# One more pair of heads turned by VectorE and through DRAM, the weights' shift also on ScalarE, and a new order

## The chip, the core and the metric

The kernel runs on one core of a Trainium2 chip. The metric is the time on the device of one execution, in microseconds; the kernel before takes 916.67 us, the median of three runs (916.0 to 917.14). A core has a matrix engine (TensorE, PE in the profile; PEld is its loading of weights), three elementwise engines (VectorE or DVE, ScalarE or ACT, GpSimd or POOL) and SyncE (SP), which issues the transfers between DRAM and the core's memory here. Each engine works through its own instructions in the order in which the program has them, and waits on semaphores for the others.

## What is computed

```python
scores = scale * np.matmul(q, k.transpose(0, 1, 3, 2))       # 8 batches, 8 heads, 576 x 576, head size 64
thresh = np.max(scores, axis=-1, keepdims=True) - tau
scores = np.where(scores >= thresh, scores, -1000000000.0)
attn = np.exp(scores - np.max(scores, axis=-1, keepdims=True))
attn = attn / (np.sum(attn, axis=-1, keepdims=True) + 1e-09)
x = heads_joined(np.matmul(attn, v))                          # 8 x 576 x 512
x_prev = shifted_by_one_position(x)
xk = mu_k * x + (1.0 - mu_k) * x_prev
xr = mu_r * x + (1.0 - mu_r) * x_prev
k = np.maximum(xk @ w_k, 0.0)                                 # 512 -> 1024
v = k * k @ w_v                                               # 1024 -> 512
out = v / (1.0 + np.exp(-(xr @ w_r)))
```

All is in 32 bit. The weights `w_k`, `w_v` and `w_r` come as 64-bit floats and are made into 32-bit ones on the chip.

## The kernel before

**Attention.** Work goes by batch `b` and by pair of heads `hp`, 0 to 3. Queries of a pair are cut into four units of 128 (`P`, both heads) and one of the last 64 queries of both heads (`T`). A unit has score matmuls (L656, or L628 and L639), then for each head a row maximum on VectorE (L740), the threshold from it (one tiny instruction on ScalarE L748, VectorE L756 or GpSimd L761), the exponential on ScalarE (L768), the mask with its sum on VectorE (L776), and a scaling by 1 / sum on GpSimd (L812) or ScalarE (L816). The probabilities `p` must then be turned so that keys lie along the partitions. There are two ways for that. In `turn_pair` and `turn_last`, a pair that isn't `moved` is turned by TensorE: 128x128 transposes (L830), 9 for a unit `P` and 5 for the unit `T`, and copies out of PSUM into `pm` (L845 on ScalarE, L846 on VectorE). A pair that is `moved` is turned in blocks of 32x32 by VectorE (L865, L878 and, for the unit `T`, L928) into `pt`, which is written to DRAM (`far`, `near`, `end`) and read back in another order into `pm`. The value matmuls (`attend`, L1017) follow: for a pair turned by TensorE once for each half of the queries, for a moved one both halves together. In the kernel before the pairs of batches 2 to 7 are moved, those of batches 0 and 1 aren't. The values `v` have one buffer.

**Feed-forward.** When four pairs are done, chunks of 256 positions go through `ffn_chunk`: mixing on GpSimd and ScalarE, matmuls with `w_k` (L1211), `w_r` (L1262) and `w_v` (L1285), each as three products of high and low parts. These matmuls are what TensorE has to do between the pieces of attention.

**Weights.** `weight` turns one of 20 pieces of 128x512 from 64 to 32 bits: GpSimd clamps the high words, ScalarE scales them (L451), VectorE shifts the low words right by 29 bits into a PSUM bank (L459) and joins the two (L467, L477), and two more steps split the result into parts for TensorE. The last shift starts at 159 us.

**Order.** All steps are first collected in a list. A table of numbers (`PLACES`) gives each step its place in one common order, from which each engine's own order and the buffers follow; another (`PICKS`) chooses, for each step that several engines can do, which one does it.

```python
eng, occ, fn = ((eng, occ, fn), *alt)[next(self.picks)]
self.out = sorted(range(len(steps)), key=place.__getitem__)
```

Of the kernel before, what the change touches and what calls it, by code (L numbers as in the profile page):

```python
# [26 lines left out]
    "!z!v!|!{#%#*#D#M#O#<#B#6#J#T#[#$#.#/#7#2#9#5#C#;#F#W#}$1$:$!$+#j#s#R#Y$J$N$O$S$V$[!/!R%W#A#U#K#V#P#X#`#f#c#i#{#~$I$T",
    "#n#x$($5$2$@#r#_#z$%$#$-#e#q#k#u$8$=$z$~$g$x$,$<$`$c%,%2%4%F%K%c!Z#?&<#S#]#t$9$4#|#o$$$.$6#y$D$K$H$P$&$3$/$7$Y${%+%B",
    "$p$t$l%8$k$n$A$X$L$R$Q$W$b$i$h$o%b%o%|&!$r%$%&%:%=%N&,&/&1&6&:&K$_%3%U%g*K%9%I%V&c()(8(^)T)q(J(i)S){*0*6*=*F*L*Q*U*W",
    "*e+D+m+r,),1,4,:,k,o,r,{-:-@.:.T*@*J*O*]*a*g*q*z+,+w-k.v-v-z-}.+.U.^.c.e.m.w/</C+4+;+>+M+V*u*|+(+C+Q,Y/Q/_/b/h0P0^0b",  # L30
    "1E1L1_0y0}1%11191G1u1{2%2T$*$e(3$m$w$}%#%(%E%S%@%L$a$d$f$j$s$q$u%7%<%M%]%f&$%}%j%p%s$v$y$|%%%!%-%*%0%)%1%.%5%?%G%P%_",
    "%r&&%T%`&E&G%>%D%6%;%H%X%R%Y%A%O%J%Q%n%v&i&l%l%w%~&?%e%k&x(#(&(-(/(T(Y%/%h))%{&+&0&H&X&T&2&8&B%Z%^%a%i%u%q%z&C&N&R&`",
    "&Z&g&d&k&n&u%t%y&%&(&#&*&-&3&.&5&7&=&f($(1(6&A&U&M&_&h&t&;&@&F&I&D&S&L&V&P&Y&W&b&q&z(A(X&{(2&s&|(](d(o(s(y(|)%);)=&O",
    "(()z(.(5(<(C(H(M(=(W(e&^&a&e&j&r&w(+(Q(v)>)L(I).(n(E(K(L(4(7&m&o(>(D(F(N&v&}(!(,(m(u)#),(_(g(:(?(j(x(V(a(;(@(h(q(r)$",
    "(G(O(P([)6)?)G)K)7)C)3)8)*)0)`*2*#(R)2+s)9)F)[)U)Z)h)n)r)u(c(f(k(w(})!)()g)o*[*c)A)P)M)Q)i)d)-)/)4):)5)B)<)D)@)I)E)O",
    ")e)l*/*<)R)Y)v)|)W)_)J)N)X)])V)c)a)p)b)k)m)t*1*R*o*}*;*>***.)}*&+],5,,1e+1,/,K,W--,7/O0U0]0e0p1g2C2O0w1$1P2!2t3)3-31",
    "3M3V3^3t3}4(4.432;2]2_2b2j3$3>3O4:4<4C4F2.222?2P2e2v3#35383B3K3Q3+333<3@3G3J3R3U3`3e3h3m3g3j3o3v4+4$4e4f4w5<5@5)5.53",
    "56595C5I5Z5x6<4U4Z4`4r4}5=5O5T5]6@*!*^-^*k+B+&+b*s,!+^+l+f)x)~*$*-*5*3*:*M+-+9+U+h+Z+I+L+O*+*8*C*E*?*G*H*X*I*V*P*_*h",
    "*m+%*p+/+5+#+*+:+=*`*f*j*l*i*w*r+$*t+7+!+<+P+X+d+i+q+{,+,<+x,$,J,d,t+++2+F+J+6+?+@+H+Y+g+_+j+u+z+~,(,?,I,8,@,0,2+v+y",
    "+S+W,%,3,.,9+a+n+k+t,F,O,S,V,Z,c,j,},^,`-/-D+N,D/A,[,i,x,y-.-E-K-Y-S+},#,&,-,;,6,>,L,b,h,z-#-%,q-9-8,E,G,A,B,M,U,R,]",  # L40
    ",H,P,N,T,m,u-,-4-C-J-G-m-=-P,e,g,_,a,l,s,v,~,f,p,n,w-(-2-;-B-R-W-]-g-V-`.8.P.X-!-$-&-+-*-3-1-5-0-7-6-?-I-M-X-_-f-|-n",
    "-s-y..-L-O->-A-T-c-[-d-F-U-Q-Z-j-o-w-r.!.*.(./.5.;.x/:-).30_.?.F.i.}/&/5.V.G.z-l-q-t-{.&.%.,.9.@.K.W.u/1.[.g.f-b-h.-",
# [1409 lines left out]
```

## Time and profile before

| | before |
|---|---|
| median of 3 runs | 916.67 us (916.0 to 917.14) |
| the profiled execution's own time | 915.72 us |
| its span, first to last instruction | 914.0 us |
| TensorE busy | 902.3 us, 99% |
| VectorE busy | 715.5 us, 78% |
| GpSimd busy | 666.5 us, 73% |
| ScalarE busy | 598.5 us, 65% |
| granted TensorE clock | 1.00 over the span |

Busy time is the time in which an engine has an instruction in work. Matmuls overlap one another, so a mean duration of one is longer than the time from one start to the next. The chain of waits is followed back from the last instruction, at each step to what released it. A line of the program (L865) is that of `kernel.py` of the run. In a transfer, the time to landing counts from its issue to its last byte.

### The profile page before, as it was taken

How to read it: one execution, taken by the hardware profiler on the slowest of the kernel's cores; microseconds unless marked ns; L12 is line 12 of the kernel's file. 1: busy time of each engine (PE TensorE's matmuls, PEld its weight loads, DVE VectorE, ACT ScalarE, POOL GpSimd, SP SyncE). 2: the span in 40 equal slices, each digit the busy share in tenths (PEclk: the TensorE clock that was granted, in tenths of full speed). 3: DMA queues.
4: the chain of work that ended last, by engine and by line, in shares of the span. 5: the costliest groups of instructions: out<-in, count | busy, mean ns of one | idle time of the engine just before them, and what ended most of it. 6: DMA issues, size and time to landing. Idle time of an engine off the chain costs nothing.

```text
span 914.0 us, 17624 instructions
## 1 busy us (share of the span) xinstructions
PE 902.3 (99%) x5970; PEld 744.1 (81%) x5970; DVE 715.5 (78%) x1615; ACT 598.5 (65%) x1154; POOL 666.5 (73%) x824
## 2 busy tenths in 40 slices
...
GB/s 332 276 217 246 105 106 119 145 305 308 334 296 311 313 320 322 301 323 313 299 297 272 315 252 321 305 321 320 296 321 291 281 310 261 238 131 24 24 24 23
DMA packets 146249, 226.60 MB, mean 248 GB/s; under 512 B 20080, under 2 KB 82672, under 8 KB 146160
## 3 DMA queue, kind: packets, MB, share of 16 engines
...
HBM read 108.27 MB, written 73.14 MB: 198 GB/s over the span
## 4 chain that ended last, share of the span: by engine, by line
PE 84%; DVE 9%; ACT 4%; issue 1%; POOL 1%; ACTq 0%; DVEq 0%; POOLq 0%
PE w L1211 21%; PE w L1285 20%; PE w L1017 15%; PE s L656 12%; PE w L1262 9%; DVE p L776 3%; DVE sm L740 3%; PE s L628 3%; PE w L830 2%; PE s L639 2%; ACT p L768 2%; ACT pm L845 1%; DVE pt L865 1%; PE w L1378 0%; DVE r L1161 0%
## 5 line engine op out<-in xcount | busy, mean ns | idle before, releaser
L768 ACT ACTIVATE p<-s,sm 128x576 f32<-128x576 f32 x288 | 209.6, 738 | 122.8 <-DVE sm L740 100.0
L776 DVE SCALAR_TENSOR_TENSOR p<-s,sm,p 128x576 f32<-128x576 f32 x288 | 230.9, 811 | 32.4 <-ACT p L768 19.7
L740 DVE TENSOR_REDUCE sm<-s 128x1 f32<-128x576 f32 x288 | 213.2, 750 | 42.4 <-PE s L656 30.4
L1211 PE MATMUL w<-xk,wk 128*128 128x256 f32 x1728 | 227.5, 281 | 0.0
L1211 PEld LDWEIGHTS w<-xk,wk 128*128 128x128 f32 x1728 | 215.8, 188 | 4.1 <-issue 1.7
L1285 PE MATMUL w<-wv,k 128*128 128x512 f32 x864 | 218.0, 395 | 0.0
L1285 PEld LDWEIGHTS w<-wv,k 128*128 128x128 f32 x864 | 157.6, 188 | 31.2 <-ACT raw L529 0.4
L1017 PE MATMUL w<-pm,v 128*64 128x256 f32 (+1 forms) x1280 | 164.9, 409 | 0.0
L1017 PEld LDWEIGHTS w<-pm,v 128*64 128x64 f32 x1280 | 88.1, 137 | 64.0 <-issue 5.8
L865 DVE STREAM_TRANSPOSE pt<-p 128x1024 f32<-128x1024 f32 x96 | 117.8, 1228 | 8.0 <-POOL p L812 5.0
L812 POOL TENSOR_SCALAR p<-p,sm 128x576 f32<-128x576 f32 x119 | 89.2, 753 | 39.0 <-DVE sm L801 36.7
L1243 POOL TENSOR_TENSOR k<-r,k 128x512 fp32r<-128x512 f32 x72 | 93.0, 1294 | 31.0 <-ACT k L1224 28.4
L816 ACT ACTIVATE p<-p,sm 128x576 f32<-128x576 f32 x133 | 101.3, 771 | 20.2 <-DVE sm L801 19.8
L1262 PE MATMUL w<-wr,xk 128*128 128x512 f32 x432 | 112.4, 395 | 0.0
L656 PE MATMUL s<-st 128*128 128x288 f32 x480 | 107.9, 308 | 1.9 <-DVE p L776 1.6
L567 POOL TENSOR_TENSOR hl<-raw,hl 128x640 fp32r<-128x640 f32 (+1 forms) x64 | 97.9, 1539 | 14.3 <-ACT hl L550 7.8
L656 PE MATMUL s<-st,st 128*128 128x288 f32 x480 | 102.2, 296 | 0.0
L656 PEld LDWEIGHTS s<-st 128*128 128x128 f32 x480 | 78.3, 189 | 20.4 <-DVE p L776 8.3
L1262 PEld LDWEIGHTS w<-wr,xk 128*128 128x128 f32 x432 | 77.5, 188 | 13.8
L656 PEld LDWEIGHTS s<-st,st 128*128 128x128 f32 x480 | 77.2, 188 | 1.9
L1220 ACT ACTIVATE r<-r 128x512 f32<-128x512 f32 x72 | 45.4, 631 | 34.8 <-DVE r L1219 33.7
L1291 DVE TENSOR_TENSOR sg<-w,sg 128x512 f32<-128x512 f32 x36 | 24.0, 680 | 44.8 <-PE w L1285 40.9
...
## 6 DMA issues: line engine op xcount, KB each, us to landing
far<-pt SPq DMA_DIRECT2D x96, 576.0 KB, 4.2
pm<-far SPq DMA_DIRECT2D x48, 1152.0 KB, 7.3
...
v<-in_v SPq DMA_DIRECT2D x36, 320.0 KB, 4.0
...
```

The lines of the kernel that those rows point to most:

```text
L567: lambda cs=cs: G.tensor_tensor(hl.get()[:, 1, cs], raw.get()[:, cs], hl.get()[:, 0, cs].bitcast(F32), op=ALU.subtract),
L656: PE.matmul(ss[y].get()[:, z, 0:HS], l.get()[:, c * P : (c + 1) * P], r[:, z * HS : (z + 1) * HS], start=(j == 0), stop=(j == 1),)
L740: lambda sv=sv, col=col: V.tensor_reduce(col(0), sv(), axis=AX.XY, op=ALU.max, negate=True),
L768: lambda sv=sv, pv=pv, col=col: A.activation(pv(), sv(), AF.Exp, bias=col(0)),
L776: lambda sv=sv, pv=pv, col=col: V.scalar_tensor_tensor(pv(), sv(), col(1), pv(), op0=ALU.is_ge, op1=ALU.mult, accum_out=col(2)),
L816: alt=[("ACT", 0.667, lambda y=y: A.activation(half(y), half(y), AF.Copy, scale=sm.get()[:, 3, y : y + 1]))],
L865: V.transpose(o, x)
L1017: PE.matmul(o[g].get()[hs, 0 : n[g]], vt.get()[:, c, hs], pt, start=(c == 0), stop=(c == 4))
L1211: PE.matmul(h.get()[:, f], l, r, start=(ct == 0 and i == 0), stop=(ct == NCT - 1 and i == 2))
L1243: lambda r=r, js=js: G.tensor_tensor(k2.get()[:, 1, js], r.get().rearrange("p (a b) -> p a b", a=2), k2.get()[:, 0, js].bitcast(F32), op=A ...
L1262: PE.matmul(z.get(), l, r, start=(ct == 0 and i == 0), stop=(ct == NCT - 1 and i == 2))
L1285: PE.matmul(vps.get(), l, r, start=(ft == 0 and i == 0), stop=(ft == NFT - 1 and i == 2))
```

## The change

The fourth pair of batch 1 (heads 6 and 7) is now among those that are moved. The shift of a weight's low words may be done by ScalarE as well: an activation that reads the words as unsigned whole numbers, multiplies by 0.936 / 2^29 and writes whole numbers. Both tables are new throughout: every step has another place, and the choices of engine are others. Sixteen of the 20 shifts are on ScalarE. The diff without the rest of the tables, of which a line each is shown:

```diff
 PLACES = (
-    "!(!!!$!#!+!,!o%x!*!)!%!&!1!=!r!}$0$C$>$G$^%C%m!.!c!n#)#1#=#E#H!w#g$U&)&9&](Z(t!2!]#G#Q#a#w$M&>!0#b&4(*(9(B(S(~#+#m#v",
...
 PICKS = (
-    "11001010001011001111000010000100002201001011000010010002000000121100002200000111000110111010101110001112100001110000",
...
+    "11101111101000010111101011101010001110112100001010000011000001100000101000021100101121000022100001001111101000000111",
...
 W_SCALE = 2.0**-112
+L_SCALE = 2.0**-29 * 0.936
...
 def moved(b, hp):
-    return b >= MOVED and hp in (0, 1, 2, 3)
+    return b >= MOVED or b == MOVED - 1 and hp >= 3
...
             reads=[(words, 0)],
             writes=[bits],
             key=key,
+            alt=[("ACT", 0.57, lambda: A.activation(bu(), words.get()[:, :, 0], AF.Copy, scale=L_SCALE))],
         )
```

Lines of the new kernel are one (up to the shift) or two (behind it) higher than those of the kernel before: L830 is L832 there, L865 is L867. The new order shows on three engines.

TensorE, before, around the second half of the attention of batch 1's fourth pair. `p_2095` are the probabilities of its last unit, `pm_281` the turned ones, `w` PSUM banks, `st` score operands, `xk` and `wk` the feed-forward's:

```order
L830 MATMUL w_97<-ident,p_2095 128x128 x4
L830 MATMUL w_100<-ident,p_2095 128x128 x4
L656 MATMUL s_124<-st_1_1992 128x288 x2
L656 MATMUL s_124<-st_1_82,st_1_1992 128x288 x2
L1211 MATMUL w_103<-xk_2074,wk_0_872 128x256 x3
L830 MATMUL w_106<-ident,p_2095 128x128
L1211 MATMUL w_103<-xk_2074,wk_0_926 128x256 x3
L656 MATMUL s_119<-st_2_2084 128x288 x2
L656 MATMUL s_119<-st_0_80,st_2_2084 128x288 x2
L1211 MATMUL w_100<-xk_2074,wk_0_564 128x256 x3
L1211 MATMUL w_103<-xk_2074,wk_0_1089 128x256 x3
L1017 MATMUL w_106<-pm_281,v_2092 64x256 x10
```

TensorE, now, up to the same pair's attention, whose values are `v_2211`:

```order
L1287 MATMUL w_99<-wv_0_2202,k_0_1184 128x512 x3
L1213 MATMUL w_108<-xk_1775,wk_0_815 128x256 x3
L658 MATMUL s_126<-st_2_2059 128x288 x2
L1213 MATMUL w_108<-xk_1775,wk_0_629 128x256 x3
L658 MATMUL s_121<-st_0_1953 128x288 x2
L658 MATMUL s_126<-st_0_80,st_2_2059 128x288 x2
L658 MATMUL s_121<-st_1_82,st_0_1953 128x288 x2
L1213 MATMUL w_108<-xk_1775,wk_0_869 128x256 x3
L1019 MATMUL w_105<-pm_192,v_2211 64x320 x10
L1019 MATMUL w_102<-pm_288,v_2211 64x256 x10
```

The nine transposes of a unit are gone, and both halves of the attention (64x320 and 64x256) stand together. From the attention of the pair before, which is not in the piece, there are 16 score matmuls (L658), 18 of L1287 and 9 of L1213 up to here.

SyncE, now, at the pair's last transfers. `far_2131` is the DRAM copy of its second half, `pt_2095` and `pt_2164` that half's two turned units:

```order
L893 DMA pm_192<-far_1997 128x4x576
L971 DMA pm_192<-end_1958 32x2x32
L887 DMA far_2131<-pt_2095 512x1x288
L595 DMA st_1_2140<-hl_2123 128x1x576
L971 DMA pm_192<-end_1958 32x2x32 x2
L887 DMA far_2131<-pt_2164 512x1x288
L523 DMA raw_2180<-in_qk 128x1280
L540 DMA v_2211<-in_v 128x640
L893 DMA pm_288<-far_2131 128x4x576
```

Before, no transfer of this pair's probabilities stood here. The pair's values are loaded between the last writing to DRAM and the last reading back.

VectorE, before, where two pieces of weights are joined (`wr` and `wv` are low words, `xT_203` the scaled high ones):

```order
L477 SCALAR_TENSOR_TENSOR xT_203<-xT_203,w_100 128x512
L740 TENSOR_REDUCE sm_1195<-s_119 128x1
L459 TENSOR_SCALAR w_100<-wr_0_419 128x512
L467 SCALAR_TENSOR_TENSOR w_100<-xT_203,w_100 128x512
L776 SCALAR_TENSOR_TENSOR p_1211,sm_1195<-s_124,sm_1195,p_1211 128x576
L477 SCALAR_TENSOR_TENSOR xT_203<-xT_203,w_100 128x512
L801 RECIPROCAL sm_1091<-sm_1091 128x1
L459 TENSOR_SCALAR w_97<-wv_0_454 128x512
```

ScalarE, now, with the shifts of two such pieces (L464 there; L452 is the scaling of the high words, L770 an exponential, L847 evictions):

```order
L770 ACTIVATE p_909<-s_121,sm_887 128x576
L750 ACTIVATE sm_887<-sm_887,small 128x1
L464 ACTIVATE w_105<-wr_0_623 128x512
L1221 ACTIVATE r_956<-w_99 128x512
L452 ACTIVATE xT_86<-wr_0_623 128x512
L531 ACTIVATE raw_881<-raw_881,small 128x640
L847 ACTIVATE xE<-w_99 128x64
L452 ACTIVATE xT_86<-wv_0_198 128x512
L464 ACTIVATE w_99<-wv_0_198 128x512
```

The shifts have gone from between VectorE's maxima and masks to ScalarE, between its exponentials and evictions.

## Rows read from the trace of the kernel before

**Rows 1.** The page's first part: busy us (share of the span) xinstructions.

```profile
PE 902.3 (99%) x5970; PEld 744.1 (81%) x5970; DVE 715.5 (78%) x1615; ACT 598.5 (65%) x1154; POOL 666.5 (73%) x824
```

**Rows 2.** Stretches: us; PE, PEld, DVE, ACT, POOL busy; clock, DMA share, GB/s.

```profile
20.00:100.00 80.00, 78.35 (x575) 57.83 (x574) 77.39 (x182) 70.84 (x169) 64.68 (x82) 1.00 0.67 230
100.00:180.00 80.00, 79.06 (x560) 62.92 (x561) 77.63 (x188) 72.65 (x158) 72.56 (x90) 1.00 0.37 125
180.00:260.00 80.00, 79.68 (x540) 67.45 (x537) 70.35 (x155) 60.36 (x112) 60.31 (x78) 1.00 0.93 311
```

**Rows 3.** Chain of waits by line: 66:193, 173:193, 193 to the end.

```profile
by line: DVE p L776 14.2%; DVE sm L740 13.4%; ACT p L768 8.9%; ACT pm L845 6.4%; PE w L1017 6.4%; PE w L830 6.3%; PE s L656 6.2%; issue 4.7%; PE w L1211 3.9%; PE w L1285 3.3%; DVE w L467 2.9%; DVE xT L477 2.9%; DVE w L459 2.9%; DVE pt L865 
by line: DVE p L776 32.0%; DVE sm L740 23.6%; DVE pt L865 16.2%; ACT p L768 7.5%; DVE sg L1291 6.0%; issue 5.2%; DVE pt L928 4.0%; ACT p L816 3.8%; DVE pt L878 3.3%; DVE sm L801 1.1%; DVE sm L756 0.7%; DVEq L776 0.1%; ACTq L768 0.1%
by line: PE w L1211 26.2%; PE w L1285 24.3%; PE w L1017 16.0%; PE s L656 13.3%; PE w L1262 12.0%; PE s L628 2.7%; issue 0.7%; DVE sm L740 0.7%; DVE p L776 0.6%; DVE r L1161 0.5%; DVE pt L865 0.5%; POOL hl L567 0.4%; POOL p L812 0.2%; POOL x
```

**Rows 4.** Pieces of the chain of waits: start us, us, what.

```profile
40.14 1.86 PE w L830 x17
151.79 0.54 PE s L656 x4
154.17 0.70 PE w L1285 x3
162.21 1.00 PE w L830 x9
173.12 0.79 DVE pt L928
193.03 0.80 PE s L656 x4
193.83 0.71 PE w L1211 x6
```

**Rows 5.** Groups: line engine op form xcount, busy us, mean ns, idle before.

```profile
L830 PE MATMUL w<-ident,p 128*128 128x128 f32 x328 | 50.5, 278 | 1.4 <-ACT pm L845 1.0
L865 DVE STREAM_TRANSPOSE pt<-p 128x1024 f32<-128x1024 f32 x96 | 117.8, 1228 | 8.0 <-POOL p L812 5.0 <-ACT p L816 2.8
L816 ACT ACTIVATE p<-p,sm 128x576 f32<-128x576 f32 x133 | 101.3, 771 | 20.2 <-DVE sm L801 19.8
L845 ACT ACTIVATE pm<-w 128x512 f32<-128x512 f32 x60 | 35.2, 598 | 1.4 <-PE w L830 1.1
L878 DVE STREAM_TRANSPOSE pt<-p 128x128 f32<-128x128 f32 x96 | 28.1, 295 | 7.2 <-POOL p L812 5.0 <-issue 1.5 <-ACT p L816 0.5
L756 DVE TENSOR_SCALAR sm<-sm,small 128x1 f32<-128x1 f32 x117 | 23.1, 202 | 0.6
L451 ACT ACTIVATE xT<-wk 128x512 f32<-128x512 f32 x8 | 5.5, 681 | 0.0
L459 DVE TENSOR_SCALAR w<-wk 128x512 uint32<-128x512 uint32 x8 | 5.5, 688 | 0.0
```

**Rows 6.** Transfers on the page: what, KB each, median us to landing.

```profile
far<-pt SPq DMA_DIRECT2D x96, 576.0 KB, 4.2
pm<-far SPq DMA_DIRECT2D x48, 1152.0 KB, 7.3
v<-in_v SPq DMA_DIRECT2D x36, 320.0 KB, 4.0
```

**Rows 7.** Timeline of SP, then of PE: start us, us, what.

```profile
197.30 3.81 SPq L891 DMA_DIRECT2D pm<-far  x2
209.00 1.30 PE L1017 MATMUL w<-pm,v 128*64 128x320 f32 x8
```

**Rows 8.** Landings of near<-pt at 179 and 202 us; waits of SP.

```profile
DMA to landing us min/median/max: 2.5/2.5/2.5
DMA to landing us min/median/max: 7.2/7.2/7.2
SPq L538 <- PE w L1017: 18.5, 9, 8.0
```

More of the change, by code (lines that the diff above doesn't have):

```diff
@@ L27 @@
[L27 to L42, printed above, removed]
@@ new lines @@
+    "1]!1!V#~!?!=!E!H!I!T!@!B!C!G!W!v#;#?!^!k!a!n!d!h!X!S!`!i!f!m!Z![!]!e!q#(#9#A!{#/!w!|!}#5#X#]#b#w#z$/!.!b$y!j!r!s!y!x",
+    "!~!z#&#%#.#2#G#|$6#>#r#B#J#D#^#-#3#4#7#8#@#:#E#C#I#h$.$A$E#e#{$!$1#O#S$]$a$d$p$t${!3#_%e#P#H#Y#g#d#k#Q#V#W#a$D$j$n$q",
+    "$B$K$Y%($<$k#j#p#q#v#u#}#y$&$#$($0$9%0%@$H$S$J$R$=$C%I%K%O%T%_%n!_#1&J#6#<#=#t#Z#R#U$%$8$*$2$4$:$;$F$>$I$G$M$^$e$v$w",
+    "%9%X%.%3%D%V$N$T$V$Z$X$`$[$b$c$l$x%C%d%w%*%8%%%;%$%+&8&:&>&B&F&Q%2%B%g(g(y%^%u%}&C&n&w)`)u)}(%(-(5(8(P(T(a(d(h(z(})$",
@@ new lines @@
+    ")2*I*d*h+C+K+N+Q+S+U+Y+b+{,#,[-.)])_)g)q)s)w)z)~*4*L.n/.,C,Q,T,Y-,-1-3-8->.s0&0B*-*3*F*N*U*>*J*e*l*q0G0U0]0b0g0x191a",
+    "1u2&2v0}1$11151d1l1p1z242>#N$5(Q$o%,$z%Q%L%G%W%)%`$h$i$m$r$u$~%-%?%F%b%q%t&.&3%o%y&!$|%#%4%7%&%1%/%6%:%A%E%N%c%x%|&)",
+    "%v&*&,&;&+&0%Y%]%=%>%a%i%l%z%H%R%P%Z&E&T&^&e&S&Y&X&r&2&W(*(/(2(F(L(U(W%5&#)N&1&<&N&b&=&k&p&U&v%f%j%m%r%~%{&%&6&P&a&f",
+    "(&(<(.&Z&u&j&$&(&/&4&-&?&7&A&9&D&L&[&h&o(:(e&M&R&~()&{(!&g&m&I&O&q(#&z(+&V&d&`&i(J(q(v({(A(K&|($(I(N))).):)?)G)W)U&_",
@@ new lines @@
+    "(6+5(?(S(G(f(r(w)%(|(j&s&t&x&}(,(0(4(=(R)9)A)C)K)S(](b(k(7(9(>(B(@(E(D(M(H(Y(O(Z(~)=)Q)V(s)#)Y)b)[)a(m(o(X(^(x),)&)4",
+    "(c(n(p)!)<)H)c)i)e)o*_*f)p)x+$+[+W(`);,A)X)h*,*0*/*?)v)|*9)1)5)7)>)O)M)d*!*T+d+j*&*G*.*=*Q*@)L)R)l)n)^)k)f)m)r*$*)*1",
+    "*Y*g*v*y+3+<*x+2*w++*(*+*8*;*:*B*A*H*D*S*P*W*`+O+f+k*[*c*r+!*k*n+r,%,!,E*Z*s+4+T+^*{,I.V.j/90=1f1w2h0i0q1<1E2y2~373=",
+    "3?3F3V3Z3n3u3}4#2u3!363C3N3^3k3x4146494<1}2!2-2O2Q2T2V2Z2d3$353;2^2l2m2n2p2r3-3/3K3P3_3e3a3h3m3|4Q4]4o4w5)5C5i4s4}51",
@@ new lines @@
+    "565J5N5S5a5q6<4H4L4T4Z4i5-5@5[656?*E*z-v+%+*+M+>+9,<,*,7,/*R*V*X*^*m*j*t+,+/+6+F+n+e+E+Z+I*}*~*b*p+(+0+-+1*|+#+&+)+D",
+    "+V+c+i,(,3,.,4,0,>+8+=+:+@+B+H+L+R+J+X+P+a+h+l+z+v,=,F,M,W,`,c,k-;-4+g+o+`+m+s+w+x+|+q+t+u+y,&,),-,5,8,K,?,N,P,a,2,6",
+    "+~,$,:,D,B,H,+,1,9,@,R,S,X,^,b,h-#-),f,z-M-`+],,.v,e,p,v-+,o-c-o-h-s,G,J,L,O,U,V,],n,w-$-K-[-b-2-C-B,g,i,Z,_,m,t,r,u",
+    ",d,j,l,q,y,|-9-!-a-x-:-D-@-V-%-*,{,}-/-5-7-<-&---0-6-F-R-Y-T-l-|-q.!-j.).H.x/C-E-H-=-A-L-U-Q-X-G-P-N-S-_-i-u-p./.6.+",
@@ new lines @@
+    ".<.%.*-e-g-Z-^-n-w-t-y-d-m-k-r.(.,.4.0.>.J.5.P.:.D.g.z-(-W1X.8.B.M.{.C/-/3/)/=-z-}-~.$.1...3.[.p.t/%/I/U/#/&/Q.#.&.;",
+    ".=.-.7.2.9.@.F.G.L.O.Q.U.Z.^.c.e.~.d.o.X._.A.E.b.i.h.l.I.K.N.R.r.w/(.}/B/N/,/8/G0%0:1W1t.Y.`.u.y.f.m.k.q/!///+/2/7/A",
+    "/H/S/T/j/_0F/^01/6/:.|/$/>/E/D/J/*/0/1/5/a/p/t0C080M0l1)0T0t1K1y.T/;2G/Y/e0#0^0V0Z/n/x0P/</?/@/F/M/K/O/V/X/]/d/h/q0K",
+    "0j0d16120s/P/R/W/[/Z/c/b/g/`/i/f/k/r/u/y/z/~0.02/s/v/l/o/{0$0!0+/w/}/|0(0/0306070@0>0E0m0,0-0004050<0;0H090?0A0D0Q0W",
@@ new lines @@
+    "0f0c0n1!1&0J0L0O0R0S0[0Y0e0X0a0`0h0y1*101.1>1=1B1b232w3d2D1U2q3l596@2{3E4(4,4B4I4r5]5g4n5%5I5M6,6I6X6]6_6d6l6r6v7278",
+    "7?6-6263686:6>6F6M6R6Z6b6o6f6i6p7*74777;7B7L7P7W7_6A6U6y6|7E7H7O7T7g7k7q7t7-7Q7V7[7b6~7%707J7~8$858:8K8Z8k8n8w9!9(9t",
+    "8(828>8P8S8c8r9$9+:)8x5p5w5y7u8~6m737Y7f7}8)818;8o848@8G8L:3:<:@:C:F:I:M:N:`:o:t:{9/959Q9]9_9b9e9h9m9q9w9}9r9u9y9{9~",
+    ":0:S:s;&;,;5;;969W9l:%:(:+:5:6:9:?:R:V:X:a:n;!;8:e:i:|;);0;e;N;Y;_;i;{<5<=<C<T=9;Q;d;m;u<$<)<.<H=+=J0*0o4h0~1:14281-",
@@ new lines @@
+    "2+2.29220p0u0v0z1#1(1+1;1N1S1c1n1h3%2}313>3,3U1,1/0k0r1317181@0w0|0{1%1H1I1Y1`1q1g1x1D1F1?1A1M1Q1P1T1C1J1L1O1e1j1o1r",
+    "2:2;2=2]1[1_1V1Z1m1s1v1{1^1k1i1|2#2%252)2C2@2M1~2(2$2*2,20212?2/26272<2A2B2`2E2i2e2t3M4+4d4P4|1G2I6G2P2[3)3r3z4*3]3g",
+    "3b2F2H2J2L2U2S2X2c2x3+393<3D4~5#4[585A4p2K2N2a2b2R2Y2W2_2g2o2j2z303@3y3w4)4%4.2f2k3(3*2s3#2|3&3.38343A3I3O3[3S3j3f3o",
+    "4S32333J3L3:3G3B3H3Q3X3W3`3i3s454!4?4@4E3R3T4$4&3Y3c3p3v4-4744484:4=4O4>4X4a4e505m6W6V6(404_8Q4{5+5=5K5_5e5F5Z5T3q3t",
@@ new lines @@
+    "3{3~424/434;4M4V4q4v4z6/6C6*646K6!4D4G4A4C4J4U4W4^4F4N4K4R4b4j4m555B5O5Q4Y4`4c4g4f4l4x5!4k4u4t4y575;5?5V5c5`5s6n5$5,",
+    "5&5(5/5:545<5*525.535G5^5d5b5x5z5|5>5H5D5E5P5W5Y5l5L5U5R5X5o5t5v5}6H6Y6^7&7h868=8|5j6=9V6D6x6N7]7X7`7d6Q7j5f5h5k5n5u",
+    "5r5{6#6%696c6j7!8[8N8A8H8T8_6&6)5~6$6.67666B6+61606;6L6P7#6g7(797<6E6J6O6T6S6a6`6h6[6k6e6q6u6z7,7F7N7M7U8,6w6{6s6t6}",
+    "7/7.757$7+7)717:7=7m7@7s7z7{767A7>7D7C7K7I7S7G7Z7R7^7n7o7|7v8#8!8+8e9::G9v9k8j93;/;y<J:,:4:};%;@;D;O;l;q;I;V;n<,<n<q",
@@ new lines @@
+    "=Z=_=a=e=g=i=m=q=x={<R<i<l<z=#=$=(=,=<=C=H=M=P=T=X=l=n=w>%>)>->3>7>J<P<Z<[<^<a<g<s<w<y<~=3=7=~>4>@>L>d=z>/>8>F>N>v>W",
+    ">^>e?8?N?R?V?c@!@)>T?-?>?A?J?_?f?k@M@_<k<D<L>0>D?F=D=V>]>q>z>}?1?@?p?$?)?2?=@*@1@7@H@N@XA%A4A=AAAGAK?s?w?}@3@4@8@F@J",
+    "@Q@]@a@fA-A1A5A>A?ADAJARAYA^AcAg?r?x?|@#@(@:@=@B@D@`@d@rANA`AdAiB-A&AEAZAmAsB`ApA}B!B)B4BcBwC+C6CeB/B:B>BiBqB{B~C%C-",
+    "Cw7l8E;T8V8b9&9<9H9@8u99947a7c7e7i7p7r7w7x7y878t8}9%9x9j:-9c9o:#8%8&8-8.8*8/8088838<898?8C8M8]8X8f8d8m8B8D8F8J8I8U8R",
@@ new lines @@
+    "8Y8O8^8W8`8z9-9E9B9I9L9O:28a8g8h8i8p8y8v9#8l8s8q8{9)9.9=9>9D9C9G90919*9,979A9F9M929;989?9S9X9^9`9i9g9|:P;.;H;G<I9J:!",
+    "=t:H:_:k:l;-;*;$;1;>9K9N9P9R9Z9Y9a:8:;:=:[:d:c;R<B;]<h<-<&9n9p9T9U9z:*:&:.9[9d9f9s:>:A:O:U:w:Z;#:$:/:7:::1:E:D:K:B:J",
+    ":L:Q:Y:q:v:x;:;9;B;o:]:^:T:W:f:p:j:r:b:h:g:m;4;7;=;A;E;C;M:z;(:u:y;+;K;2;L:~;6;<;?;[;`;b;j;v;~<%<Q=6=o=r>g;3;c?,;w<V",
+    "<4<`=%=)<m<9<u;F;J;P;S;^;X;a;s;}<!<2<@<7>B=O=[>M>=>E;U;W;g;h;Z;p;f;r;k;|;t<(</<;<A<><f<d<r;x;z<1<3<#<+<*<0<6<E<<<F<K",
@@ new lines @@
+    "<S<j<c<t<{=!=b<W<Y<8<:<]<b<e<o<?<M<G<O<v=0=>=4=B=E=G<N<U<x<|<X<_<p<}=&=2=-=5=;=?=A=@=K=U=Y>(>n?l?K?G=.=hA<>&>S><>_>i",
+    ">o>r>X>a=*=/=1=8===:=F=N=S=`>2>Q>9?0?(?Z?y?U?6=p=s=I=L=v>!=|>$=]=j=d=k>*>1>:>5>O>H>V=Q=R=u=y=W=c=^=f=}>#>+>6>c>f>j>h",
+    ">x>w>|?b>,>.>>>?>;>G>A>I>C>Y>K>Z>`>k?#>m?%?4?<>P>R>b>l>U>s>[>t>p>y>u>{?!?.?;?B?M?L?T?n@[B0B8@w@V@nA:B6BY@sASAeAzB@BH",
+    "BOBsC!BVBmBtBzC:CICXCfCrCuC}D$D(D,D3D8C2CACZCcCoCyC~D&DNDSDVDqC=C@CMCRC^CmD)D*D9DADFDHC5CGCHCUD0D2D5D=DBDGDMD]DZDjDr",
```

157 lines of the change are left out of this document (65 added, 92 removed).

## The prediction

> **What bounds the kernel now.** I read the share of busy time first, then the same by stretches, then the chain of waits, and last the groups of instructions. TensorE is busy for 902.3 us of the 914.0 us span [rows 1], so the first thought is that whatever leaves TensorE leaves the time. The stretches make this finer [rows 2]: from 20 to 180 us VectorE is busy for 77.39 + 77.63 = 155.0 us of 160, ScalarE for 143.5, TensorE for 157.4; from 180 us on TensorE has all of its time (79.68 of 80) and VectorE has room (70.35 of 80). The reader is to see two regimes. Early, while the softmax of batches 0 and 1 and the preparation of the weights run together, VectorE and TensorE are both full; later TensorE alone is.
>
> The chain of waits says where they hand over. Between 66 and 193 us it runs through VectorE's mask (14.2%) and maximum (13.4%), ScalarE's exponential (8.9%), evictions (6.4%) and TensorE's pieces in turn; from 173 to 193 it is VectorE's for nearly all of the time, and from 193 on the lines with a share worth the name are TensorE's matmuls [rows 3]. The last hand-over is the scores at 193.03 us, behind a mask of VectorE [rows 4]. So the end is "the time at which VectorE lets TensorE pass the first heads of batch 2" plus "TensorE's work that is left then". A gain must shorten one of the two.
>
> **The change part by part.** The sum is made against the profiled execution, 915.72 us (span 914.0 and 1.7 us around it); the median of the runs is 916.67, 0.95 higher, and I add that at the end.
>
> TensorE loses the turning of one pair of heads: 4 units of 9 transposes and one of 5, 41 of 128x128. Seventeen in a row take 1.86 us and nine take 1.00 [rows 4], 0.11 us each, so 41 x 0.11 = 4.5 us. The group's busy time over its count, 50.5 / 328 = 0.154 us [rows 5], holds waits as well and gives the upper end, 6.3 us. I take 4.5, since the chain shows pieces without waits. The number of score, value and feed-forward matmuls stays, so 4.5 us is what TensorE can give back.
>
> VectorE loses 16 of the 20 shifts at 0.688 us [rows 5], -11.0 us, and they count: they are 2.9% of the chain's 127 us between 66 and 193 us, 3.7 us [rows 3]. It gains four large block turns at 1.228, four small ones at 0.295 and one of 0.79 [rows 4, 5], +6.9 us. By the choices of engine in the two orders, batches 0 and 1 also get 17 more thresholds on VectorE (0.202 each [rows 5], +3.4), and a few evictions and one ReLU change sides (-0.1). That is -0.8 us in all: VectorE's early load, the one that is at 97%, hardly changes.
>
> ScalarE gains 16 shifts. The trace has none there; the nearest row is its scaling of the high words, same shape and stride, at 0.681 us [rows 5], which I take: +10.9 us. Below, nothing; above, perhaps twice that if unsigned input were slow, 21.8 us. It loses nine evictions of 512 columns at 0.598 and seven scalings of probabilities at 0.771, -10.8 us [rows 5], and smaller evictions and 16 thresholds besides, which I put at 0.2 to 0.3 each, -5 us or more. So ScalarE's early load falls by some 5 us even with the shifts. At twice the price it would rise by 6 us, into 16 us in which ScalarE is idle early [rows 2]. GpSimd gains those seven scalings, which I put at about the same each, +5 us, beside 64.68 + 72.56 = 137 of 160 us busy early [rows 2]; that is hidden. The rest of the order's new choices lie after 190 us, where VectorE, ScalarE and GpSimd wait for TensorE, and cost nothing while that holds.
>
> The way through DRAM adds 14 transfers on SP's queue in a stretch whose DMA share is 0.37 [rows 2], so bandwidth is there. What counts is delay: the pair's attention now waits for the writing (4.2 us at the median) and the reading back (7.3 us) [rows 6] in place of an eviction. In the new order both halves of the pair's attention stand together, at the place of the former second half, and the last leg before it is the tightest. The value tile has one buffer, so its load waits for the attention of the pair before; behind it on SP stands the second read-back. TensorE has 16 score matmuls, 18 feed-forward ones of 512 columns and 9 of 256 to do between the two attentions. Four score matmuls take 0.54, three of 512 take 0.70 and six of 256 take 0.71 [rows 4], so the leg is 2.2 + 4.2 + 1.1 = 7.5 us. The issue of the values (some 0.5) and the read-back (7.3) make 7.8. So a wait of 0 to 2 us, of which I take 0.6, and 0.4 more for the first pair of batch 2, whose attention in the kernel before started at 209.00 us; its read-backs were issued from 197.30 on, the second some 3.4 us later [rows 7], so that one of 7.3 us leaves under 1 us.
>
> How long the read-back takes depends on the traffic: a transfer of 256 KB landed after 2.5 us at 179 us and after 7.2 us at 202 us [rows 8]. The Trainium skill, "DMA: Bandwidth & Descriptors", section "Latency and other measured facts", says the same in its way: the access time of HBM is 0.2 us on the average and 2 us under high load. By this rule the read-back of batch 1 would be quicker than the median row, the wait nil and the sum the full 4.5 us.
>
> A rule also bears on VectorE's price. The Trainium skill, "VectorE: DVE Perf Modes", section "The three transpose paths", has TensorE at 390 ns and VectorE at 311 ns for a 128x128 turn in bf16, VectorE in 32x32 blocks only. By that ratio VectorE would pay 3.6 us for the 4.5 that TensorE saves, and its early load would fall by 4 us. The rows say 1.228 us for eight such squares, 0.154 each against 0.11 on TensorE [rows 4, 5], in fp32; the measurement decides, and VectorE pays 6.9.
>
> Sum: -4.5 + 0.6 + 0.4 = -3.5 us; 915.72 - 3.5 = 912.2, and with 0.95 for the median **913.2 us**.
>
> **The rivals.**
> *VectorE still sets the pace (no change).* Its work until the hand-over falls by 0.8 us only. If it idles as much as before (5 us of 160 [rows 2]), the first attention of batch 2 comes 0.8 us earlier, and the time that TensorE has won is spent waiting for it: 916.67 - 0.8 = 915.9. For it speaks that the chain from 173 us to the hand-over is nearly all VectorE [rows 3]. Against it: shifts and evictions that VectorE and ScalarE waited on in the chain leave it, and the first feed-forward matmuls stand earlier in TensorE's order, so it has other work meanwhile.
> *The read-back is late and stalls TensorE (slower).* In the new order the pair's last block turn stands at place 322 of VectorE, after as much work as the kernel before has done at about 173 us, where its block turn of 0.79 us stands [rows 4]. If VectorE gets no quicker, 173.1 + 4.2 + 7.3 + 1 for two issues = 185.6 us, while TensorE's remaining work is then what it was at 183.9 in the trace of before: 1.7 us slower. If the reading back also queues behind the value load (4.0 us [rows 6]) and the waits of SP for TensorE that the trace has (18.5 us in 9 pieces [rows 8]) repeat here, the 4 us count too: 916.67 + 1.7 + 4.0 = 922 at the worst, and 920 between the two. It decides when the read-back is issued later than 4 us ahead of the attention. Against it: the light DMA traffic there, and that ScalarE's lower load lets VectorE idle less.
> *More than the transposes goes (faster still).* The idle time of TensorE from 20 to 180 us is 2.6 us [rows 2]. With feed-forward work available earlier it could go: 916.67 - 4.5 - 2.6 = 909.6. Against it: the waits sit at scores that need VectorE.
>
> **How the numbers follow.** The forecast, most of TensorE's 4.5 us arriving with up to 2 us of new waits, holds 911 to 914.8 and gets 0.53; the larger gain 0.12; no change 0.20; the late read-back 0.15. Less than 0.2% (1.8 us) can't be told from no change in this kernel, so faster means under 914.8 and slower over 918.5. Faster: 0.53 + 0.12 = 0.65; same 0.20; slower 0.15. The range goes from 909.5 (the larger gain) to 918.8 (no change, and a part of the late read-back, with the shift's unknown price on ScalarE); the forecast's own is 911 to 914.8.
>
> **What would show it.** In the profile of the changed kernel: 287 transposes and TensorE's busy time down by 4 to 6 us; VectorE from 20 to 180 us still at 95% or more; shifts on ScalarE at about 0.68 us; the chain handing over to TensorE some 3 to 5 us earlier than 193 us for the same work; at the pair's attention and at the first one of batch 2 waits for a read-back of under 1 us each. The prediction is wrong if TensorE waits there for several us, if the hand-over comes no earlier, or if the shift on ScalarE takes over 1 us and the exponentials queue behind it.

## The result: slower, and the profile after

| | before | changed |
|---|---|---|
| median of the runs (us) | 916.34 (915.53 to 917.14, 4 runs) | 928.25 (927.47 to 930.68, 4 runs) |
| profiled execution: span (us) | 914.0 | 926.3 |
| TensorE busy (us), instructions | 902.3, 5970 | 906.1, 5929 |

The ratio is 1.0136, 95% interval 1.0124 to 1.0149: 12 us slower, where 3.5 us faster was forecast.

The page's first part of the changed kernel (busy us, share, instructions), against [rows 1]:

```profile
PE 906.1 (98%) x5929; PEld 744.7 (80%) x5929; DVE 716.5 (77%) x1622; ACT 592.6 (64%) x1147; POOL 671.4 (72%) x817
```

The 41 transposes are gone (5970 to 5929), and yet TensorE is busy for 3.8 us more; its idle time rises by 8.5 us (from 914.0 - 902.3 = 11.7 to 926.3 - 906.1 = 20.2). At 0.11 us each the transposes would have taken 4.5 off, so the work that is left took 8.3 us longer. Some of that is a lower clock, as shown below. The stretches of [rows 2], and then three short ones (us; PE, PEld, DVE, ACT, POOL busy; granted clock, DMA share, GB/s):

```profile
20.00:100.00 80.00, 78.69 (x562) 57.38 (x562) 76.81 (x186) 72.86 (x167) 69.44 (x84) 1.00 0.65 223
100.00:180.00 80.00, 71.97 (x497) 56.42 (x493) 74.82 (x180) 68.31 (x140) 65.35 (x86) 0.96 0.49 165
180.00:260.00 80.00, 79.06 (x534) 65.34 (x535) 71.91 (x157) 51.41 (x104) 61.30 (x77) 1.00 0.95 317
145.00:163.00 18.00, 11.08 (x76) 8.98 (x73) 17.04 (x44) 16.20 (x34) 14.99 (x21) 0.90 0.39 132
155.00:160.00 5.00, 2.08 (x13) 1.42 (x11) 4.77 (x12) 4.34 (x9) 4.62 (x8) 0.93 0.32 111
160.00:165.00 5.00, 3.13 (x14) 2.79 (x14) 4.51 (x10) 4.05 (x11) 3.34 (x6) 0.50 0.62 202
```

Before, TensorE had work for 79.06 us of 100 to 180; now for 71.97, and the hole lies between 145 and 163 us, where it works for 11.08 us of 18 while VectorE does for 17.04. What it waits for, from 145 to 170 us and from 186 to 222 (us in total, times, longest):

```profile
PE s L658 <- DVE p L778: 6.9, 4, 2.9
...
PE s L658 <- DMA st<-hl: 0.8, 1, 0.8
```

The chain of waits shows how (start us, us, what; the first line is from the full stretch before it):

```profile
107.64 2.84 PE w L1019 x20
...
154.56 1.32 DVE sm L742 x2
155.88 0.68 DVE pt L930
156.60 0.84 DVE p L778 x2
157.48 1.55 PE s L658 x8
159.07 0.76 POOL p L814
...
160.15 0.87 issue
161.03 0.80 DVE p L778 x2
161.87 2.29 PE s L658 x8
164.16 0.85 PE w L832 x4
165.01 3.43 PE w L1019 x20
168.44 1.26 PE s L658 x8
...
172.87 0.44 PE w L832 x4
```

Scores wait for the masks that free their banks; a block turn (L930, L867) stands between maxima and masks. Behind the hole the same work takes longer: eight scores 2.29 against 1.26 us, four transposes 0.85 against 0.44, twenty value matmuls 3.43 against 2.84, 2.0 us in all for these three. The granted clock is 0.50 from 160 to 165 us (the lower level, 1.2 GHz), after a stretch in which TensorE was busy for 2.08 of 5 us.

No read-back is waited for. The two attentions in question, by TensorE's timeline, start with nothing idle ahead of them, at 190.73 and (209.00 in [rows 7]) 216.12 us:

```profile
190.73 5.07 PE L1019 MATMUL w<-pm,v 128*64 128x320 f32 x40
...
216.12 5.07 PE L1019 MATMUL w<-pm,v 128*64 128x320 f32 x40
```

The groups that answer to [rows 5] (busy us, mean ns):

```profile
L832 PE MATMUL w<-ident,p 128*128 128x128 f32 x287 | 44.3, 283 | 0.3 <-ACT xT L847 0.2
L464 ACT ACTIVATE w<-wv 128x512 uint32<-128x512 uint32 x7 | 4.7, 664 | 0.0
L867 DVE STREAM_TRANSPOSE pt<-p 128x1024 f32<-128x1024 f32 x100 | 122.7, 1227 | 6.7 <-ACT p L818 2.6 <-DMA far<-pt 1.9 <-POOL p L814 1.9
```

The reading that matters most compares one point of the program: the first maximum over the last unit of batch 2's first pair. It starts at 185.14 us before and at 190.23 now. All that the engines did up to it, before:

```profile
0.00:185.10 185.10, 179.89 (x1260) 137.90 (x1260) 173.46 (x410) 159.12 (x359) 144.28 (x187) 1.00 0.56 195
```

and in the changed kernel:

```profile
0.00:190.20 190.20, 178.22 (x1205) 135.62 (x1206) 173.28 (x420) 159.54 (x341) 147.92 (x194) 0.97 0.62 215
```

VectorE's work up to there is the same, 173.5 and 173.3 us; its idle time is 185.1 - 173.5 = 11.6 and 190.2 - 173.3 = 16.9 us. It comes 5.1 us late, all of it idle time.

### The profile page after: what moved, and what is told of

Read it like the earlier page. It is cut to its first block, busy times and chain, and to the rows that moved or that the text cites. A ratio compares the mean times of both kernels' runs of the same rounds, so it can differ in the third digit from the quotient of the medians.

```text
span 926.3 us, 17533 instructions
## 1 busy us (share of the span) xinstructions
PE 906.1 (98%) x5929; PEld 744.7 (80%) x5929; DVE 716.5 (77%) x1622; ACT 592.6 (64%) x1147; POOL 671.4 (72%) x817
## 4 chain that ended last, share of the span: by engine, by line
PE 88%; DVE 7%; issue 2%; POOL 1%; ACT 1%; DMA 1%; SPq 0%; POOLq 0%; DVEq 0%; ACTq 0%
PE w L1213 21%; PE w L1287 19%; PE w L1019 16%; PE s L658 14%; PE w L1264 10%; PE s L630 3%; PE w L832 3%; DVE p L778 2%; DVE sm L742 2%; PE s L641 1%; DVE r L1163 1%; DVE pt L867 1%; PE w L1380 1%; DMA st<-hl 1%; ACT p L770 1%
## 5 line engine op out<-in xcount | busy, mean ns | idle before, releaser
L770 ACT ACTIVATE p<-s,sm 128x576 f32<-128x576 f32 x288 | 209.8, 738 | 137.7 <-DVE sm L742 98.0
L1213 PE MATMUL w<-xk,wk 128*128 128x256 f32 x1728 | 230.9, 282 | 0.0
L1213 PEld LDWEIGHTS w<-xk,wk 128*128 128x128 f32 x1728 | 219.1, 189 | 3.7 <-issue 0.9
L1287 PE MATMUL w<-wv,k 128*128 128x512 f32 x864 | 217.7, 395 | 0.0
L1287 PEld LDWEIGHTS w<-wv,k 128*128 128x128 f32 x864 | 157.7, 188 | 32.1 <-issue 0.8
L867 DVE STREAM_TRANSPOSE pt<-p 128x1024 f32<-128x1024 f32 x100 | 122.7, 1227 | 6.7 <-ACT p L818 2.6
L814 POOL TENSOR_SCALAR p<-p,sm 128x576 f32<-128x576 f32 x130 | 96.7, 747 | 38.0 <-DVE sm L803 35.7
L658 PE MATMUL s<-st 128*128 128x288 f32 x480 | 109.8, 312 | 11.0 <-DVE p L778 10.1
L658 PEld LDWEIGHTS s<-st 128*128 128x128 f32 x480 | 77.9, 189 | 35.3 <-DVE p L778 20.1
L818 ACT ACTIVATE p<-p,sm 128x576 f32<-128x576 f32 x122 | 91.7, 769 | 17.2 <-DVE sm L803 16.7
L658 PE MATMUL s<-st,st 128*128 128x288 f32 x480 | 102.1, 298 | 0.0
L658 PEld LDWEIGHTS s<-st,st 128*128 128x128 f32 x480 | 77.3, 189 | 2.5 <-issue 0.6
```

The costliest lines, as they stand in the source:

```text
L658: PE.matmul(ss[y].get()[:, z, 0:HS], l.get()[:, c * P : (c + 1) * P], r[:, z * HS : (z + 1) * HS], start=(j == 0), stop=(j == 1),)
L770: lambda sv=sv, pv=pv, col=col: A.activation(pv(), sv(), AF.Exp, bias=col(0)),
L814: lambda y=y: G.tensor_scalar(half(y), half(y), sm.get()[:, 3, y : y + 1], 0.0, op0=ALU.mult, op1=ALU.add),
L867: V.transpose(o, x)
L1213: PE.matmul(h.get()[:, f], l, r, start=(ct == 0 and i == 0), stop=(ct == NCT - 1 and i == 2))
L1287: PE.matmul(vps.get(), l, r, start=(ft == 0 and i == 0), stop=(ft == NFT - 1 and i == 2))
```

## The experiments

Four theories are weighed. A: VectorE's load up to the hand-over sets the end. B: TensorE, VectorE and ScalarE are all near the bound there, so what one loses gives nothing and what one gains is paid. P: VectorE alone sets the pace from 145 to 195 us. F: TensorE only lacks work in the hole. All times are medians, beside medians of 916.1 to 916.4 us of the kernel before on the same chip; the ratio to it stands with its 95% interval. The old order is that of the kernel before, the new order that of the changed kernel.

**The parts, in the old order.** First the shifts alone:

```diff
+L_SCALE = 2.0**-29 * 0.936
...
             key=key,
+            alt=[("ACT", 0.57, lambda: A.activation(bu(), words.get()[:, :, 0], AF.Copy, scale=L_SCALE))],
```

> The kernel before with one edit: the same 16 shifts of low words run on ScalarE, nothing else is moved. Theory A (VectorE's load up to the hand-over sets the end, so relief of VectorE shortens it): 16 x 0.69 us leave VectorE, 3 to 7 us arrive, 909 to 914 us. Theory B (the two engines hand each other work in a fixed order, and work put between ScalarE's exponentials delays VectorE's masks): 16 x 0.55 us more on ScalarE in its busiest stretch, 920 to 926 us.

920.74 us, 1.0047 (1.0032 to 1.0062): theory B. The relief of VectorE is real and worth nothing:

```profile
0.00:189.80 189.80, 181.76 (x1260) 137.44 (x1261) 165.91 (x396) 166.70 (x375) 144.38 (x187) 1.00 0.55 190
60.00:100.00 40.00, 38.24 (x281) 28.43 (x282) 34.93 (x79) 39.22 (x97) 33.44 (x40) 1.00 0.53 179
100.00:140.00 40.00, 38.09 (x270) 30.13 (x270) 35.24 (x85) 38.93 (x86) 34.61 (x45) 1.00 0.34 114
```

The point of 185.1 us comes at 189.8, with VectorE's work down to 165.9 and its idle time up to 23.9. From 60 to 140 us ScalarE is busy for 78.15 of 80 us, VectorE for 70.17; in the kernel before they were at

```profile
60.00:100.00 40.00, 38.97 (x290) 29.59 (x290) 39.19 (x88) 38.53 (x95) 34.25 (x41) 1.00 0.55 181
100.00:140.00 40.00, 39.26 (x285) 31.05 (x285) 39.01 (x93) 38.63 (x88) 37.07 (x47) 1.00 0.36 121
```

77.16 and 78.20: both full. VectorE now waits (60 to 140 us) for joins and exponentials behind ScalarE, and for scores:

```profile
DVE sm L742 <- PE s L658: 2.8, 6, 0.8
DVE w L469 <- ACT w L464: 2.3, 2, 1.4
DVE p L778 <- ACT p L770: 1.8, 6, 0.8
```

Then the pair's move alone:

```diff
 def moved(b, hp):
-    return b >= MOVED and hp in (0, 1, 2, 3)
+    return b >= MOVED or b == MOVED - 1 and hp >= 3
```

> The pair's move alone: old order and old engines (all 20 shifts on VectorE), with the fourth pair of batch 1 turned by VectorE and through DRAM. The new steps stand behind the softmax of their unit, the pair's attention stands where its second half stood, and the DMA issues of this pair and of batch 2's first pairs, and the attention's three evictions, are set to where their data are ready. If taking 41 transposes from TensorE is worth its 4.5 us, 912 to 916 us. If VectorE sets the pace between 145 and 195 us (theory P), 6.9 us of block turns land on it and the attention waits for the way through DRAM: 921 to 931 us.

928.66 us, 1.0139 (1.0124 to 1.0154): as much as the whole change.

```profile
0.00:192.70 192.70, 179.12 (x1199) 137.00 (x1200) 178.63 (x419) 155.07 (x345) 143.85 (x187) 0.96 0.61 209
...
180.00:185.00 5.00, 2.48 (x12) 2.08 (x12) 4.93 (x12) 3.63 (x8) 5.00 (x6) 0.80 0.86 242
185.00:190.00 5.00, 2.99 (x10) 2.37 (x10) 4.41 (x11) 1.40 (x3) 1.97 (x3) 0.50 1.04 363
```

The point comes at 192.7 us: VectorE's work is 5.2 us up, its idle time 2.4. From 145 to 200 us (SP: from 150) TensorE waits for masks, VectorE for the writing of a turned tile, and SP stands behind transfers whose data are not ready:

```profile
PE s L658 <- DVE p L778: 9.4, 6, 3.0
...
DVE pt L867 <- DMA far<-pt: 1.8, 1, 1.8
...
SPq L595 <- ACT hl L552: 9.4, 1, 9.4
SPq L887 <- DVE pt L880: 6.8, 2, 6.1
```

Both edits together:

> Both parts of the change in the old order: the pair moved as in pair_moved_old_order, and the 16 shifts on ScalarE as in old_order_shift_scalare. If VectorE's work up to the hand-over is what counts (the forecast's account), the shifts' relief pays for the block turns and the time is 916 to 921 us. If TensorE, VectorE and ScalarE are all close to the bound before 195 us, so that work taken from one gives nothing and work added to one is paid (theory B), both losses add: 916.3 + 12.3 + 4.4 = 933, 929 to 935 us.

933.98 us, 1.0191 (1.0163 to 1.0220): the losses add (4.4 + 12.3 = 16.7; 17.5 measured). VectorE's relief does not pay for its turns. The two kernels differ in more than the shifts: 328 steps between about 145 and 200 us have another place than with the move alone, most of them by at most four.

**What the pair's move is made of.** The kernel before, with the pair's transposes done twice, or partly left out:

```diff
-            for c, x in enumerate(ins):
+            for c, x in [*enumerate(ins)] * times:
...
-            for c, x in enumerate(ins):
+            for c, x in enumerate(ins[:n]):
```

> The kernel before with one edit: TensorE turns the probabilities of batch 1's fourth pair twice, 41 transposes of 0.11 us more, 4.5 us, at the places where the change takes 41 away. If TensorE's work there counts in full (the first term of the forecast), 920 to 922 us. If VectorE sets the pace there (theory P), the 4.5 us lie in TensorE's waits or delay a mask a little: 916 to 918 us.

921.39 us, 1.0057 (1.0042 to 1.0072): 5.1 us, paid in full: in the old order theory P falls here.

> The kernel before with 27 of the 41 transposes of batch 1's fourth pair left out (of a group of four or of the last unit only the first is done; what is evicted then is partly stale). TensorE has 27 x 0.11 = 3.0 us less to do at the place where the change takes 4.5 away. If that is worth its time (first term of the forecast), 913 to 914 us. If VectorE and ScalarE hold TensorE there anyway (theory B), 915 to 917 us.

915.69 us, 0.9998 (0.9989 to 1.0007): nothing. TensorE's waits for masks from 145 to 200 us grow to 1.0 us (second line), from 0.2 before (first line):

```profile
PE s L656 <- DVE p L776: 0.2, 1, 0.2
...
PE s L656 <- DVE p L776: 1.0, 3, 0.4
```

The copies out of PSUM stay in this kernel; leaving them out as well was not tried.

Then VectorE's side, without the transfers:

```diff
-            lambda: V.reciprocal(sm.get()[:, 3, ysl], sm.get()[:, 2, ysl]),
+            lambda: (
+                V.reciprocal(sm.get()[:, 3, ysl], sm.get()[:, 2, ysl]),
+                unit["job"]["b"] == 1 and unit["job"]["hp"] == 3 and spare(unit),
+            ),
```

> The kernel before, and VectorE also does the moved pair's block turns, into a tile that nobody reads: 4 x 1.23 + 4 x 0.295 + 0.77 = 6.9 us behind the reciprocals of its units. TensorE still does its transposes, nothing goes through DRAM. If the turns are what makes the moved pair slow, 922 to 925 us. If it is the way through DRAM and the later attention, 916 to 919 us.

921.96 us, 1.0070 (1.0053 to 1.0086): 5.9 us for 6.9 us of turns. That is their price at this place: here they stand ahead of the scaling of the probabilities, in the moved pair behind it. From 155 to 185 us scalings on GpSimd (L826) and ScalarE (L830) wait for them:

```profile
POOL p L826 <- DVE pt L719: 3.4, 3, 2.3
...
ACT p L830 <- DVE pt L719: 2.2, 2, 1.6
```

> Both edits: VectorE does the moved pair's block turns into a tile that nobody reads, and TensorE leaves 27 of its 41 transposes out; nothing goes through DRAM and the attention stands where it stood. If the work that changes engine explains the 12.3 us of pair_moved_old_order, 924 to 928 us. If the way through DRAM and the attention's later place make most of it, 916 to 920 us.

923.00 us, 1.0077 (1.0062 to 1.0092), between the two expectations: 6.9 us. Leaving TensorE's transposes out does not pay for the turns either. The rest of the pair's 12.3 us, 5.4, comes with the way through DRAM, the attention's later place, the places that the pair's steps were given, and the last 14 transposes and the evictions that go with them; it was not divided further. The clock is in it too. With the pair moved, the granted clock is below 1.00 in the two short rows above and in these three:

```profile
165.00:170.00 5.00, 3.06 (x9) 2.68 (x10) 4.48 (x11) 2.87 (x5) 4.66 (x5) 0.59 0.90 278
170.00:175.00 5.00, 5.00 (x21) 4.22 (x20) 3.75 (x8) 2.52 (x5) 4.45 (x7) 0.73 1.01 358
...
190.00:195.00 5.00, 5.00 (x26) 4.54 (x25) 4.25 (x8) 1.21 (x3) 2.66 (x6) 0.68 0.94 302
```

TensorE's busy time times the missing share of the clock gives 6.2 us over the five rows, an estimate of what the lower clock took. With the turns alone no row of 5 us up to 260 us is below 1.00, and without the way through DRAM one is (0.66 from 165 to 170). So the clock, behind longer waits for masks, could make up the whole rest; how much of it reaches the end is not shown. Transfers as such are waited for little in that trace, 1.8 us by VectorE and 0.3 by TensorE.

**The new order.** Shifts back on VectorE, by their 16 entries in PICKS:

> The changed kernel with one edit: all 20 shifts on VectorE again, the new order kept. If the shifts on ScalarE are what makes the new kernel slow, 918 to 924 us. If VectorE's load in the first 190 us sets the end, 11 us come back to it and 4 to 9 of them arrive: 932 to 937 us.

932.98 us, 1.0200 (1.0157 to 1.0243): in this order, which is made for them, the shifts on ScalarE are worth 4.7 us, as theory A has it. Next, two kernels that change from one order to the other on the way:

> The changed kernel, but the first 1100 steps of the kernel before stand in the old order with their old engines (shifts on VectorE); from there on, about 147 us, the rest follows in the new order, with the moved pair. If the loss comes from the moved pair and the order behind 147 us, it stays: 924 to 929 us. If it comes from the early order (shifts on ScalarE, other choices of engine), it goes: 914 to 918 us.

928.28 us, 1.0128 (1.0113 to 1.0143): the same as the changed kernel, so the loss is there without the early order. That the early order costs nothing does not follow: where the two orders meet, TensorE waits 3.0 us for a scaling on GpSimd, a wait that neither order has there by itself:

```profile
PE w L832 <- POOL p L814: 3.0, 1, 3.0
```

> The changed kernel up to its step 1600 (about 220 us, behind the first attention of batch 2), and the rest in the old order with the old choices of engine. The lag against the kernel before grows by 4.7 us behind 220 us in the changed kernel (7.6 us of TensorE work at 260 us, 12.3 at the end). If that is the new order of the later batches, it goes: 922 to 925 us. If it follows from the late start of batch 2, it stays: 927 to 930 us.

925.37 us, 1.0100 (1.0083 to 1.0118), between the two expectations: 2.9 us of the change's 11.9 go with the new order of the later batches, and 9 remain. No run undoes the pair's move inside the new order, so what the move costs there is not measured by itself.

**The hole at 145 to 163 us.** Seven feed-forward pieces into it; on TensorE:

```diff
+L1287 MATMUL w_102<-wv_0_1144,k_0_1184 128x512 x3
 L832 MATMUL w_108<-ident,p_1821 128x128 x4
...
+L1287 MATMUL w_102<-wv_0_1120,k_0_1184 128x512 x3
...
-L1287 MATMUL w_102<-wv_0_1144,k_0_1184 128x512 x3
-L1287 MATMUL w_102<-wv_0_1120,k_0_1184 128x512 x3
```

> The changed kernel with seven feed-forward pieces (21 matmuls of 512 columns, 4.9 us) moved from 169 to 190 us into the stretch of 153 to 163 us where TensorE waits, with the scalings, squares and three evictions that they need. If TensorE only lacks work there (theory F), the 4.9 us and some 2 us of the halved clock come back: 921 to 923 us. If VectorE's pace sets the hand-over (theory P), TensorE waits for the scores behind 170 us instead, and at most the halved clock's 2 us come back: 926 to 929 us.

929.89 us, 1.0145 (1.0130 to 1.0161): against theory F, and no better than the changed kernel. It is 0.9 us above P's range, but the waits move as P has it: the hole is filled and opens again later, where TensorE now has too little. The clock falls behind it there as well (0.66 from 175 to 180 us):

```profile
155.00:160.00 5.00, 3.96 (x26) 3.51 (x26) 4.41 (x11) 3.48 (x9) 4.26 (x7) 1.00 0.01 2
170.00:175.00 5.00, 2.59 (x20) 1.59 (x16) 5.00 (x13) 3.76 (x8) 1.83 (x4) 1.00 0.89 297
180.00:185.00 5.00, 3.97 (x26) 3.11 (x27) 5.00 (x11) 3.52 (x8) 4.95 (x4) 1.00 0.87 310
```

Useless work into it, 6 new steps of four transposes and the third pair's done twice:

```diff
+    for j in range(STIR):
+        pt = psum("w", [P, 4, P], 4)
...
+            lambda pt=pt: [PE.transpose(pt.get()[:, c, :], ident.get(), ident.get()) for c in range(4)],
```

> The changed kernel with useless work in TensorE's idle stretch: batch 1's third pair is turned twice (41 transposes, 4.5 us, 147 to 173 us) and 24 transposes of the identity (2.6 us) stand in front of the scores at 161.9 us. If VectorE sets the pace there (theory P), these 7.1 us cost nothing or little, and if they keep the clock from falling to 0.50 at 160 us, up to 2.5 us come back: 925 to 930 us. If TensorE's own work sets the time there, all of it is paid: 933 to 936 us.

931.65 us, 1.0170 (1.0154 to 1.0187): a miss of both, 3.4 us paid for 7.1. The clock fell all the same, so the 24 transposes took 4.29 us, not 2.6, and held up the scores behind them; what the clock alone costs stays open.

```profile
159.99 4.29 PE w L1391 x24
```

VectorE's large turns twice:

```diff
                 V.transpose(o, x)
+                if job["b"] < MOVED:
+                    V.transpose(o, x)
```

> The changed kernel with the four large block turns of the moved pair done twice: 4 x 1.23 = 4.9 us more on VectorE between 159 and 196 us. If VectorE's time between two masks is what TensorE waits for there, 3 to 6 us: 931 to 935 us. If the turns lie beside the exponentials (VectorE sits idle for 4 to 5 us between 145 and 190 us), 928 to 930 us.

931.84 us, 1.0174 (1.0153 to 1.0195): 3.6 us for 4.9 of turns, so its time between two masks counts although it sits idle for some of it.

**Another order.** Two orders searched with the durations of the traces; only PLACES differs.

> The changed kernel with another order of its steps 100 to 1450 (to about 200 us), searched for an earlier end of TensorE's work there; work and engines are unchanged. If the loss is one of order alone, it goes down to 914 to 918 us. If the moved pair's block turns and its way through DRAM cost by themselves, about half stays: 920 to 925 us.

933.50 us, 1.0180 (1.0154 to 1.0206).

> The kernel before with its steps 100 to 1450 searched in the same way; work and engines are unchanged. TensorE is busy for 157.4 of the 160 us from 20 to 180 us, so at most 2.6 us can go: 913 to 916 us. If the search only fits its own table of durations, no gain or a loss: 916 to 919 us.

927.25 us, 1.0115 (1.0089 to 1.0142). Both are misses, slower than what they start from: this search, by the durations of single instructions, found no better order, so it does not show whether there is one. No version here beats the kernel before.

## Why the prediction was wrong, step by step

Two steps failed. The forecast's own sign of being wrong shows it: the hand-over came 5.1 us later, not 3 to 5 earlier.

**The first term, -4.5 us for 41 transposes, is the first step that failed.** Its size was right (0.11 us each; done twice they cost 5.1). But taking 27 of them away, 3.0 us, was worth 0.2 us by the ratio (-0.6 to 1.0). I read TensorE's 157.4 busy us of 160 in [rows 2] as room that would come back, beside VectorE's 155.0 in the same row. With two engines at 97 and 98% and handing each other every score, work added to either was paid in the old order (5.1, 5.9 us), and work taken from one was not returned.

**VectorE's sum, -0.8 us, is the second: right in size (173.5 to 173.3 us of work up to the same point) and wrong in what followed.** The shifts' -11.0 "count", it says, and in the old order they do not: alone they cost 4.4 us. In the new order, made for them, they are worth 4.7. The 6.9 us of turns do count, 5.9 us. Netting the one against the other was the error: many of the shifts go from a stretch (60 to 140 us) in which ScalarE was as full as VectorE, and the turns come between 155 and 180 us.

**ScalarE.** The shift's price was right: 0.66 us against the 0.681 taken. That ScalarE's early load would fall by 5 us was wrong: 159.1 and 159.5 us up to the same point. GpSimd's +5 was nearly right (144.3 to 147.9) and was hidden.

**The way through DRAM.** A wait of 0.6 us at the pair's attention and 0.4 at batch 2's first were forecast; there were none. The light traffic that the prediction counted on (a DMA share of 0.37) was not there: while the last read-back was under way, from 183.8 to 191.6 us, the share was 0.97. It landed 7.8 us after its issue at 183.81 us, when the attention's first half was running. So the rule of the Trainium skill ("DMA: Bandwidth & Descriptors", "Latency and other measured facts") by which it would be quicker under light load was not put to the test here. What was missed is what stands around it: operands of batch 2 landed 0.8 us late for their scores, and in the old order the transfers, the later attention, the lower clock and what else goes with them made 5.4 us.

**The block turns.** By the ratio in the Trainium skill ("VectorE: DVE Perf Modes", "The three transpose paths") they would be cheaper than TensorE's transposes. That ratio is for bf16. The rows, in fp32, have it the other way, before and after (1.227 us for eight squares against 8 x 0.11). And 6.9 us of them cost 5.9 us of the whole time, while the transposes that they replace return nothing.

**The rivals.** "VectorE still sets the pace" had the right engine and the wrong time: it kept VectorE's idle time at 5 us, which grew by 5.3. The late read-back had the right sign for a wrong reason. None had the pair's block turns as a loss by themselves.

**The sum as measured:** 4.4 for the shifts, 12.3 for the pair (5.9 of it the turns alone), 17.5 together in the old order; the new order takes 5.7 of that back, 934.0 to 928.3. Of the pair's 12.3, the 5.4 beyond the turns and the 27 transposes stay open.
